# Column transform of a two-axis DFT computed for half of the rows, the mirrored rows summed from the same PSUM tiles read backwards

## The chip, the cores and the metric

The kernel runs on one core of one Trainium2 chip. The metric is the device time of one execution in microseconds (us), the median of three runs. TensorE is called PE below, VectorE DVE, ScalarE ACT, GpSimd POOL and SyncE SP. ACT, POOL and SP also issue DMAs[...].

## The reference, cut to what matters

Chunked attention (32 rows a chunk, 16 rows of left and 8 of right context, 8 memory rows) gives x of shape 4 x 768 x 512. A Fourier mixing and an MLP follow:

```
X = np.fft.fft(x, axis=1)
X = np.fft.fft(X, axis=2)
mixed = np.real(X).astype(np.float32)
u = x + mixed
mu = np.mean(u, axis=-1, keepdims=True)
var = np.mean((u - mu) ** 2, axis=-1, keepdims=True)
un = (u - mu) / np.sqrt(var + 1e-06)
ch = np.maximum(un @ w_ch1, 0.0) @ w_ch2
return (u + ch).astype(np.float32)
```

x is real, so row 768-k of `mixed` is row k with its 512 columns read as j -> (512-j) mod 512. The change rests on this.

## The kernel before, in words

A batch b (0 to 3) is 768 rows, six tiles of 128 rows, held in `xsb` (three buffers, so batch 3 waits until batch 0 is written out). Each batch has four attention units (two heads each), in all sixteen units n = 0 to 15. One unit loads q, k and v (`e_load_q` L242, `e_load_k` L247, `e_load_v` L252, all on SP), casts q and k (`e_cast_q` L270, `e_cast_k` L274: on DVE in batch 0, on POOL afterwards), copies the overlapping v rows (`e_overlap` L278, POOL), transposes on PE (L286, L302), takes scores (`e_scores` L316), exponentials on ACT (L331), values (`e_values` L335) and normalises into `xsb` on DVE (`e_norm` L351). The q, k and v buffers are for three units.

When a batch's x is complete, the row transform follows: folds on DVE (`zy`, `pq`, `ff`, L371 to L388), a split into a high and a low fp16 part (L396 on ACT, L401 on DVE), matmuls with cosine and sine tables (`ps`, L411), and a second split into `up` (L423 on ACT, L427 on DVE). `up` holds the 385 rows 0 to 384. `e_dn` (L430) copies it backwards on DVE into `dn`, which gives rows 384 to 767. The column transform is `e_columns` (L435): eight matmuls of 256 columns for each of six row tiles, from `up` for tiles 0 to 2 and from `dn`, with the sine table of the other sign, for tiles 3 to 5. `e_sum` (L447) adds the result to x in place; then come the statistics (L455, L456), `un` on ACT (L461), a transpose (`tp`, L468) and `unT` on DVE (L473), tile by tile.

The MLP of a batch runs in two halves of three tiles: sixteen blocks `ph` (L489, four matmuls each, one ReLU L496 on ACT each), then three blocks `pc` (L503, sixteen matmuls each), the sum `osb` on DVE (L509) and a store issued from ACT (`e_out` L512). The first `ph` of a half needs the three `unT` of that half. The two `ph`/`pc` PSUM buffers (`mlp`) alternate; `acc`, with two buffers as well, is shared by `ps`, `pm` and `tp`. The 4 MB of MLP weights are loaded by eight DMAs from POOL (L637, L639) once unit 3 is done.

What comes when is decided before the kernel is built: class `Plan` walks through all tasks with a hand-written cost each, gives every engine the first task by rank whose inputs and buffers are free at that planned time, and emits the tasks in the order so found. On the chip every engine then takes its instructions strictly in that order. MLP tasks have the lowest rank (`MLPS`), so PE takes them when it plans nothing else. SP takes its tasks in rank order and stops at the first that isn't ready.

Of the kernel before, what the change touches and what calls it, by code (L numbers as in the profile page):

```python
# [34 lines left out]
class Plan:  # L35
# [10 lines left out]
    def add(self, engine, cost, emit, after=(), take=(), give=(), rank=None, moved=0.0):  # L46
        t = dict(engine=engine, cost=cost, emit=emit, after=[a for a in after if a is not None],
                 take=take, give=give, rank=len(self.tasks) if rank is None else rank,
                 moved=moved, done=None, at=None, no=len(self.tasks))
        self.tasks.append(t)  # L50
        return t

    def order(self):
# [8 lines left out]
        while any(waiting.values()):  # L62
# [4 lines left out]
            for e, ts_ in waiting.items():  # L67
                if idle.get(e, 0.0) > now:
                    continue
                for t in ts_:  # L70
                    if any(a["done"] is None or a["end" if a["engine"] == e else "done"] > now
                           for a in t["after"]):
                        if e == "SP":
                            break
                        continue
                    need = {}
                    for tag in t["take"]:
                        need[tag] = need.get(tag, 0) + 1
                    if any(self.free[tag] < m for tag, m in need.items()):
                        if e == "SP":  # L80
                            break
                        continue
                    for tag in t["take"]:
                        self.free[tag] -= 1
                    cost = t["cost"] * (2.0 if e == "PE" and now < 40.0 else 1.0)
                    idle[e] = t["end"] = now + cost
                    if t["moved"]:
                        wire = max(wire, now + cost) + t["moved"]
                        t["done"] = t["end"] = wire + self.LAG["DMA"]
                    else:  # L90
                        t["done"] = now + cost + self.LAG.get(e, 0.07)
                    for tag in t["give"]:
                        gives.append((t["done"], tag))
                    t["at"] = now
                    placed.append(t)
                    ts_.remove(t)
                    moved = True
                    break
# [11 lines left out]
def kernel(  # L110
# [35 lines left out]
    fpool = ctx.enter_context(tc.tile_pool(name="fx", bufs=1))  # L146
    aps = ctx.enter_context(tc.tile_pool(name="attn_ps", bufs=1, space=bass.MemoryType.PSUM))
# [15 lines left out]
                     xsb=3, fold=2, hl=1, up=4, dn=4, acc=2, mlp=2, un=3, unT=2, hT=1, osb=3))  # L163
# [24 lines left out]
    NEG = -BIGM / 8.0  # L188
    cosS = wpool.tile([P, 2, 3, NK], FP16)
# [3 lines left out]
    sinD = wpool.tile([P, 2, HD], FP16)  # L193
# [225 lines left out]
    def e_up(b, par, ab):  # L419

        up = fpool.tile([P, 2, NK, 2], FP16, tag="up", bufs=4, name="up")
        up_of[b, par, ab] = [up.rearrange("p i k s -> p i (k s)"), None, up]
        nc.scalar.copy(up[:, 0].rearrange("p k s -> p s k"), ps_of[b, par, ab])  # L423

    def e_rest(b, par, ab):
        up = up_of[b, par, ab][2]
        nc.vector.tensor_tensor(up[:, 1].rearrange("p k s -> p s k"), ps_of.pop((b, par, ab)),  # L427
                                up[:, 0].rearrange("p k s -> p s k"), ALU.subtract)

    def e_dn(b, par, ab):  # L430
        dn = fpool.tile([P, 2, HS], FP16, tag="dn", bufs=4, name="dn")
        nc.vector.tensor_copy(dn, rev_ap(up_of[b, par, ab][2], HS, HS, [[2 * NK, 2]]))
        up_of[b, par, ab][1] = dn

    def e_columns(b, kt):  # L435
        pm_of[b, kt] = pm = fps.tile([P, 2, HD], FP32, tag="acc", name="pm")
        for par in range(2):
            im = 0
            for ab in range(2):
                rhs = cosD if ab == 0 else (nsinD if kt < 3 else sinD)  # L440
                for part in range(2):
                    lhs = up_of[b, par, ab][kt // 3][:, part, ts(kt % 3, P)]
                    nc.tensor.matmul(pm[:, par, :], lhs, rhs[:, par, :],  # L443
                                     start=(im == 0), stop=(im == 3))
                    im += 1

    def e_sum(b, kt):  # L447
        uv = xs[b][:, kt, :].rearrange("p (j c) -> p c j", c=2)
        nc.vector.tensor_tensor(uv, pm_of.pop((b, kt)), uv, ALU.add)  # L449

    def e_stats(b, kt):
# [3 lines left out]
        nc.vector.bn_stats(st6, xs[b][:, kt, :])  # L455
        nc.vector.bn_aggr(mu_of[b][:, kt, :], st6)  # L456

    def e_un(b, kt):
        un_of[b, kt] = un = fpool.tile([P, DM], FP16, tag="un", bufs=3, name="un")

        nc.scalar.activation(un, xs[b][:, kt, :], AFT.Identity, bias=mu_of[b][:, kt, 0:1],  # L461
# [17 lines left out]


# [25 lines left out]
    def e_osb(b, sh, stl):  # L506
# [3 lines left out]
                                       xs[b][:, st, :], ALU.mult, ALU.add)  # L510

    def e_out(b, st):  # L512
        nc.scalar.dma_start(out[b, ts(st, P), :], osb_of.pop((b, st)))


# [40 lines left out]
    t_norm = {}  # L556

# [53 lines left out]
    def e_sines(par):  # L611
# [4 lines left out]
        else:  # L616
            nc.scalar.activation(nsinD, rD, AFT.Sin, bias=0.0, scale=-scD)
            nc.scalar.activation(sinD, rD, AFT.Sin, bias=0.0, scale=scD)
            nc.scalar.activation(cosD, yD, AFT.Sin, bias=hpi_b, scale=-scD)

    def e_table_rows():

        for tab, par, s0 in ((nsinD, 0, 1.0), (sinD, 0, 1.0), (nsinD, 1, -1.0), (sinD, 1, 1.0)):
# [7 lines left out]
    t_sines = add("ACT", 6.2, e_all_sines, [t_angle["S"], t_angle["D"], x_last])  # L631
    t_rows = add("DVE", 1.3, e_table_rows, [t_sines])
# [10 lines left out]
    def fourier(b):  # L643
        nrm = [[t_norm[b * HP + i, g] for i in ii for g in range(2)] for ii in ((0, 1), (2, 3))]
        t_rest, t_dn = {}, {}
# [25 lines left out]
        for par in range(2):  # L671
            for ab in range(2):
                t_dn[par, ab] = add("DVE", 0.36, lambda par=par, ab=ab: e_dn(b, par, ab),
                                    [t_rest[par, ab]], take=("dn",))
# [4 lines left out]
        def columns(kt):  # L679
            cols[kt] = add("PE", 0.9, lambda: e_columns(b, kt),  # L680
                           allr + [t_rows] + (list(t_dn.values()) if kt > 2 else []),
                           take=("acc",),
                           give=("up",) * 4 if kt == 2 else ("dn",) * 4 if kt == 5 else ())
# [3 lines left out]
        for kt in range(NST):  # L687
            if kt + 1 < NST:
                columns(kt + 1)
            su = add("DVE", 0.7, lambda kt=kt: e_sum(b, kt), [cols[kt]], give=("acc",))  # L690
            sa = add("DVE", 0.9, lambda kt=kt: e_stats(b, kt), [su, sa])
            un = add("ACT", 0.72, lambda kt=kt: e_un(b, kt), [sa], take=("un",))
            tp = add("PE", 0.26, lambda kt=kt: e_turn_u(b, kt), [un, t_idh], take=("acc",),
                     give=("un",))
            t_un[kt] = add("DVE", 0.43, lambda kt=kt: e_unT(b, kt), [tp, t_un.get(kt - 1)],
                           take=("unT",) if kt == 0 else (), give=("acc",))
# [5 lines left out]
    def mlp(b, t_un, rs):  # L702
        for sh in range(2):
# [11 lines left out]
            for stl in range(3):  # L715
# [12 lines left out]
                add("ACT", 0.1, lambda st=st: e_out(b, st), [os_], give=("osb",), moved=0.9,  # L728
# [46 lines left out]
```

The softmax here doesn't subtract the row's maximum and nothing guards it: scores larger than these inputs give would overflow.

## Time and profile before

| what | us |
|---|---|
| three runs | 342.72, 344.65, 345.95; median 344.65 |
| span of the profiled execution | 342.6 |
| PE busy in it | 292.4 (85%) |
| DVE, ACT, POOL busy | 190.6, 168.9, 82.2 |
| matmuls `pm` (L443) | 192 of 256 columns |
| DVE copies `dn` (L432) | 16 of 455 ns, 7.1 |
| first `ph` of batch 0 (L489) starts | 77.98 |
| last DMA of the loads before the traffic ebbs | about 88 |

The median of the runs is 2.05 us above the span of the profile. PE, PEld (its weight loads) and the other engines overlap, so busy times don't add up to the span; a group's "idle before" is the time its engine stood still just ahead of it, with what ended that.

### The profile page before, as it was taken

To read this page: it belongs to the slowest core of one execution; us is meant where nothing else is said; L and a number is where in the kernel's file an instruction comes from. 1 tells how busy PE (TensorE), PEld (TensorE's weight loads), DVE (VectorE), ACT (ScalarE), POOL (GpSimd) and SP (SyncE) were. 2 spreads that over 40 slices of the span, in tenths; PEclk is the share of its full clock that TensorE was granted. 3 is DMA by queue.
4 is the path that set the end of the run, shared out by engine and by line. 5 is a ranking of instruction groups with operands and counts; after the bars stand their busy time and mean duration, and the time that the engine had idled before them with its cause. 6 is when DMAs were issued, how large, how long until landed. Compare 5 with 4: busy or idle time off the path is not lost.

```text
span 342.6 us, 6911 instructions
## 1 busy us (share of the span) xinstructions
PE 292.4 (85%) x2833; PEld 188.3 (55%) x2833; DVE 190.6 (56%) x374; ACT 168.9 (49%) x297; POOL 82.2 (24%) x89
## 2 busy tenths in 40 slices
PE   0678647959998886859999998699999999999995
PEld 0567535837555575637765665565645454554542
DVE  6954497958079999799793459860720100101001
ACT  7554784656737458674632733347226053160620
POOL 6534694233442736362001100000010000000000
PEclk9999999969999999998999999699999999999999
DMA  7999999999505893670002300010020100201001
GB/s 157 209 176 164 158 230 205 217 168 174 83 0 148 140 186 96 181 170 2 2 0 92 56 2 0 31 63 0 0 95 0 63 31 0 92 2 61 33 31 61
DMA packets 42046, 30.65 MB, mean 89 GB/s; under 512 B 30240, under 2 KB 32288, under 8 KB 42016
## 3 DMA queue, kind: packets, MB, share of 16 engines
q1 hardware_dynamic: 35584, 19.67, 32.5%
q0 software_dynamic: 2688, 4.19, 6.7%
q10 hardware_dynamic: 3744, 6.36, 4.8%
q8 instruction: 22, 0.36, 0.5%
q14 instruction: 8, 0.07, 0.1%
HBM read 28.11 MB, written 6.29 MB: 100 GB/s over the span
## 4 chain that ended last, share of the span: by engine, by line
PE 63%; DVE 16%; DMA 8%; SPq 3%; ACT 3%; issue 3%; POOL 3%; ACTq 0%; POOLq 0%
PE ph L489 23%; PE pc L503 22%; PE xa L347 6%; DMA qf<-in_q_dram 5%; PE pm L443 5%; PE ps L411 4%; DMA kf<-in_k_dram 2%; SPq L259 2%; DVE lo L401 2%; DVE zy L371 1%; PE tp L468 1%; DVE pq L379 1%; ACT e L331 1%; PE sc L323 1%; DVE xsb L358 1%
## 5 line engine op out<-in xcount | busy, mean ns | idle before, releaser
L496 ACT ACTIVATE hT<-ph 128x384 f16<-128x384 f32 x128 | 61.1, 492 | 73.2 <-PE ph L489 71.8
L489 PE MATMUL ph<-unT,w_sb 128*128 128x384 f16 x512 | 91.2, 326 | 1.4 <-ACT hT L496 0.8
L503 PE MATMUL pc<-w_sb,hT 128*128 128x512 f16 x384 | 88.3, 381 | 0.0
L489 PEld LDWEIGHTS <-w_sb 128*128 128x128 f16 x512 | 48.4, 97 | 36.8 <-issue 6.5
L509 DVE SCALAR_TENSOR_TENSOR osb<-pc,rstd,xsb 128x512 f32<-128x512 f32 x24 | 17.9, 748 | 83.2 <-PE pc L503 83.2
L503 PEld LDWEIGHTS <-hT 128*128 128x128 f16 x384 | 36.8, 98 | 40.0 <-issue 0.7
L280 POOL COPY va<-va 32x780 f32<-32x780 f32 x32 | 37.4, 1177 | 48.3 <-DMA va<-in_v_dram 40.8
L331 ACT ACTIVATE e<-sc,mbias 128x384 f32<-128x384 f32 x64 | 33.7, 579 | 22.5 <-PE sc L323 21.2
L347 PE MATMUL xa<-va,e 128*64 128x65 f32 x768 | 34.6, 250 | 7.9 <-ACT e L331 3.7
L347 PEld LDWEIGHTS xa<-va,e 128*64 128x64 f32 x768 | 29.9, 159 | 14.7 <-issue 7.2
L461 ACT ACTIVATE un<-xsb,mu_s 128x512 f16<-128x512 f32 x24 | 17.3, 722 | 22.4 <-DVE mu_s L456 22.3
L357 DVE RECIPROCAL zs<-xa 128x6 f32<-128x6 f32 x32 | 6.1, 192 | 32.7 <-PE xa L347 32.7
L477 POOL TENSOR_SCALAR rstd<-mu_s 128x6 f32<-128x6 f32 x4 | 1.0, 242 | 96.9 <-DVE osb L509 89.5
L323 PE MATMUL sc<-qT,kTb 64*128 64x64 bf16 x384 | 12.7, 206 | 11.8 <-ACT kTb L312 10.5
L423 ACT CAST up<-ps 128x386 f16<-128x386 f32 x16 | 9.7, 605 | 20.9 <-PE ps L411 19.5
L411 PE MATMUL ps<-cosS,hi 128*128 128x193 f16 (+1 forms) x72 | 16.8, 284 | 3.2 <-DVE ff L388 3.2
L411 PE MATMUL ps<-cosS,lo 128*128 128x193 f16 (+1 forms) x72 | 16.5, 284 | 3.1 <-DVE lo L401 3.1
L449 DVE TENSOR_TENSOR xsb<-pm,xsb 128x512 f32<-128x512 f32 x24 | 16.3, 678 | 4.1 <-PE pm L443 3.9
L358 DVE TENSOR_TENSOR xsb<-xa,zs 128x384 f32<-128x384 f32 x32 | 17.8, 558 | 1.1
L401 DVE TENSOR_TENSOR lo<-ff,hi 128x768 f16<-128x768 f32 x16 | 17.3, 1103 | 1.5 <-ACT hi L396 1.4
L323 PEld LDWEIGHTS <-kTb 64*128 64x128 bf16 x384 | 8.7, 103 | 17.1 <-ACT kTb L312 11.7
L396 ACT CAST hi<-ff 128x768 f16<-128x768 f32 x16 | 13.1, 832 | 9.8 <-DVE ff L388 9.7
(90 smaller groups left out, 374.6 us busy)
## 6 DMA issues: line engine op xcount, KB each, us to landing
qf<-in_q_dram SPq DMA_DIRECT2D x16, 384.0 KB, 4.2
kf<-in_k_dram SPq DMA_DIRECT2D x16, 384.0 KB, 4.1
out_dram<-osb ACTq DMA_DIRECT2D x24, 256.0 KB, 2.0
va<-in_v_dram SPq DMA_DIRECT2D x32, 144.0 KB, 4.7
w_sb<-in_moe_w_ch_dram POOLq DMA_DIRECT2D x8, 512.0 KB, 16.8
va<-in_v_dram SPq DMA_DIRECT2D x32, 48.0 KB, 7.2
va<-in_mem_v_dram SPq DMA_DIRECT2D x32, 24.0 KB
mkf<-in_mem_k_dram ACTq DMA_DIRECT2D x2, 32.0 KB, 3.7
```

The source lines that it names most:

```text
L280: nc.gpsimd.tensor_copy(v1[96:128, 0:NT, 0:D + 1], v1[0:32, 1:NB, 0:D + 1])
L323: nc.tensor.matmul(sc[:, hh, t6, :], kT[r0:r0 + 64, t * BS:t * BS + P], qT[r0:r0 + 64, ts(t, 64)], start=True, stop=True, tile_position=(r ...
L331: nc.scalar.activation(e1[:, :, :, ts(half, 32)], sc[:, :, 0:6, ts(half, 32)], AFT.Exp, bias=mbias[:, half:half + 1], scale=1.0 / math.sqr ...
L347: nc.tensor.matmul(xa[64 * half:64 * half + 64, st, hh, 0:65], e1[:, hh, t6, :], v1[:, 6 * g + t6, 0:65], start=True, stop=True)
L358: nc.vector.tensor_tensor(xs[b][:, 3 * g:3 * g + 3, 2 * pr * D:(2 * pr + 2) * D] .rearrange("p s (h d) -> p s h d", h=2), xa[:, :, :, 0:D] ...
L401: nc.vector.tensor_tensor(lo[:, ab].rearrange(fl), ff_of[b, par][:, ab].rearrange(fl), hi[:, ab].rearrange(fl), ALU.subtract)
L411: nc.tensor.matmul(out_[:, sp, :], part[:, ab, sp * 3 + st, c0:c1], tab[:, sp, st, :], start=(st == 0 and i == 0), stop=(st == 2 and i == 1))
L461: nc.scalar.activation(un, xs[b][:, kt, :], AFT.Identity, bias=mu_of[b][:, kt, 0:1], scale=-1.0)
L489: nc.tensor.matmul(ph[:, 0:384], w1_sb[:, dt, ts(ht, P)], unT_of[b][:, dt, sh * 384:(sh + 1) * 384], start=(dt == 0), stop=(dt == NDT - 1))
L496: nc.scalar.activation(hT_of[b, sh][:, ht, :], ph_of.pop((b, sh, ht))[:, 0:384], AFT.Relu, bias=0.0, scale=-1.0)
L503: nc.tensor.matmul(pc_of[b, sh, stl], hT_of[b, sh][:, ht, ts(stl, P)], w2_sb[:, ht, :], start=(ht == 0), stop=(ht == NHT - 1))
L509: nc.vector.scalar_tensor_tensor(osb, pc_of.pop((b, sh, stl)), rstd_of[b][:, st:st + 1], xs[b][:, st, :], ALU.mult, ALU.add)
```

## The change

- `columns` runs for three row tiles (m = 0 to 2), not six. `e_dn` and its buffers go, and so do the table `sinD`, its ACT instruction and four of the eight memsets on DVE.
- `e_middle` is new: eight matmuls with one column of weights, for row 384 alone.
- Mirrored tiles 3 to 5 take the `pm` of tile 0 to 2 backwards in `e_sum`, plus a one-column add for column 0, and for the first of them a one-row add for row 384. Row p of such a tile is now row 768 - 128 m - p of the output.
- x of those rows is brought into that order through DRAM: `e_mirror_out` stores tiles 3 to 5 of `xsb` (0.79 MB) from SP, `e_mirror_in` gathers them by three indexed DMAs from POOL into `xr` (one buffer). The index tile is built once on POOL (`e_turn`).
- Half of the output stores become scatters from POOL.
- Tiles are worked in the order KT = 0, 3, 1, 4, 5, 2. SP tasks marked `loose` may overtake a blocked SP task in the plan.

```diff
@@ class Plan, order()
+                held = False
                 for t in ts_:
+                    if held and not t["loose"]:
+                        continue
...
-                        if e == "SP":
-                            break
+                        held = held or (e == "SP" and not t["loose"])
                         continue
@@ column transform
-    def e_dn(b, par, ab):
-        dn = fpool.tile([P, 2, HS], FP16, tag="dn", bufs=4, name="dn")
-        nc.vector.tensor_copy(dn, rev_ap(up_of[b, par, ab][2], HS, HS, [[2 * NK, 2]]))
-        up_of[b, par, ab][1] = dn
+    def e_mirror_out(b):
+        fold_dram[b] = dr = dpool.tile([HS, DM], FP32, tag=f"mirror{b}", name=f"mirror{b}")
+        nc.sync.dma_start(dr.rearrange("(m p) d -> p m d", p=P), xs[b][:, 3:6, :])
+
+    def e_mirror_in(b):
+        xr_of[b] = xr = fpool.tile([P, 3, DM], FP32, tag="xr", bufs=1, name="xr")
+        for m in range(3):
+            nc.gpsimd.indirect_dma_start(
+                xr[:, m, :], None, fold_dram[b],
+                bass.IndirectOffsetOnAxis(ap=turn[:, 0, m:m + 1], axis=0))
...
+    def e_middle(b):
+        pm_of[b, 3] = pm = fps.tile([P, 2, HD], FP32, tag="acc", name="pm")
+        for par in range(2):
+            im = 0
+            for ab in range(2):
+                rhs = cosD if ab == 0 else nsinD
+                for part in range(2):
+                    nc.tensor.matmul(pm[0:1, par, :], up_of[b, par, ab][0][:, part, HS:HS + 1],
+                                     rhs[:, par, :], start=(im == 0), stop=(im == 3))
+                    im += 1
...
     def e_sum(b, kt):
-        uv = xs[b][:, kt, :].rearrange("p (j c) -> p c j", c=2)
-        nc.vector.tensor_tensor(uv, pm_of.pop((b, kt)), uv, ALU.add)
+        m = kt % 3
+        if kt < 3:
+            uv = xs[b][:, kt, :].rearrange(cj, c=2)
+            nc.vector.tensor_tensor(uv, pm_of[b, m], uv, ALU.add)
+            return
+        xr, pm = xr_of[b], pm_of[b, m]
+        turned = bass.AP(tensor=pm.tensor, offset=pm.offset + HD,
+                         ap=[list(pm.ap[0]), [HD - 1, 2], [-1, HD]])
+        nc.vector.tensor_tensor(xs[b][:, kt, :].rearrange(cj, c=2), turned,
+                                xr[:, m, :].rearrange(cj, c=2), ALU.add)
+        nc.vector.tensor_tensor(xs[b][:, kt, 0:1], pm[:, 0, 0:1], xr[:, m, 0:1], ALU.add)
+        if m == 0:
+            nc.vector.tensor_tensor(xs[b][0:1, kt, :].rearrange(cj, c=2),
+                                    pm_of.pop((b, 3))[0:1],
+                                    xr[0:1, m, :].rearrange(cj, c=2), ALU.add)
@@ stores
     def e_out(b, st):
-        nc.scalar.dma_start(out[b, ts(st, P), :], osb_of.pop((b, st)))
+        osb, kt = osb_of.pop((b, st)), KT[st]
+        if kt < 3:
+            nc.scalar.dma_start(out[b, ts(kt, P), :], osb)
+            return
+        nc.gpsimd.indirect_dma_start(
+            out.rearrange("b s d -> (b s) d"),
+            bass.IndirectOffsetOnAxis(ap=turn[:, 1 + b, kt - 3:kt - 2], axis=0), osb, None)
@@ fourier(b)
-        for par in range(2):
-            for ab in range(2):
-                t_dn[par, ab] = add("DVE", 0.36, lambda par=par, ab=ab: e_dn(b, par, ab),
-                                    [t_rest[par, ab]], take=("dn",))
+        mo = add("SP", 0.35, lambda: e_mirror_out(b), nrm[0] + nrm[1], moved=2.6, loose=True)
+        mi = add("POOL", 3.0, lambda: e_mirror_in(b), [mo, t_turn], take=("xr",), moved=2.6)
...
         columns(0)
-        for kt in range(NST):
-            if kt + 1 < NST:
-                columns(kt + 1)
-            su = add("DVE", 0.7, lambda kt=kt: e_sum(b, kt), [cols[kt]], give=("acc",))
+        cols[3] = add("PE", 0.7, lambda: e_middle(b), [cols[0]], take=("acc",))
+        for i, kt in enumerate(KT):
+            if kt == 3:
+                columns(1)
+            if kt == 4:
+                columns(2)
+            m = kt % 3
+            more = [] if kt < 3 else [mi] + ([cols[3]] if m == 0 else [])
+            su = add("DVE", 0.7 if kt < 3 else 1.5 if m == 0 else 0.8, lambda kt=kt: e_sum(b, kt),
+                     [cols[m]] + more,
+                     give={0: (), 1: (), 3: ("acc", "acc"), 4: ("acc",), 5: ("xr",),
+                           2: ("acc",)}[kt])
```

## The prediction

> **What bounds the kernel now.** I read the page's busy line first, then PE's busy time by stage, then the timeline of the first 100 us with the DMA view. PE is busy for 85% of the span, and time ends with it:
>
> ```profile
> PE 292.4 (85%) x2833; PEld 188.3 (55%) x2833; DVE 190.6 (56%) x374; ACT 168.9 (49%) x297; POOL 82.2 (24%) x89
> ```
>
> So span = PE's work + PE's idle time: 292.4 + 50.2 = 342.6. The stages show where it idles (columns: stretch, its length, busy time of each engine, clock, DMA share, GB/s):
>
> ```profile
> 0.00:78.20 78.20, 48.46 (x694) 39.92 (x695) 55.10 (x138) 48.06 (x72) 38.98 (x47) 0.96 1.10 187
> 78.20:135.60 57.40, 51.97 (x680) 35.39 (x678) 45.51 (x83) 34.65 (x60) 26.38 (x27) 1.00 0.64 119
> 135.60:175.00 39.40, 33.34 (x400) 24.59 (x397) 34.67 (x58) 24.47 (x44) 11.98 (x10) 0.96 0.32 78
> 175.00:202.80 27.80, 27.61 (x328) 16.94 (x326) 13.89 (x30) 13.10 (x26) 3.25 (x4) 1.00 0.17 46
> 202.80:229.00 26.20, 21.96 (x145) 14.30 (x143) 23.35 (x40) 8.19 (x13) 0.00 (x0) 0.87 0.05 21
> 229.00:342.60 113.60, 109.09 (x596) 57.20 (x595) 18.12 (x31) 40.38 (x83) 1.59 (x2) 0.99 0.10 38
> ```
>
> Idle: 29.7, 5.4, 6.1, 0.2, 4.2, 4.5. Six tenths of it lies ahead of 78.2, where the MLP of batch 0 starts. Until then PE has only attention and one row transform, and these wait for loads: the DMA share is 1.10. After 78.2 there is always MLP work to fill with. PE's timeline around that point (start, length, what, [idle before]):
>
> ```profile
> 73.58 0.82 PE L286 MATMUL trq<-ident_b,qb 96*128 96x96 bf16 x8 [3.73 <-POOL qb L272]
> ...
> 77.98 1.02 PE L489 MATMUL ph<-unT,w_sb 128*128 128x384 f16 x4
> ```
>
> The first waits for the q of unit 7; the second is the first MLP block. In the DMA view for 55 to 60 us the queue of POOL (weights, q0) and that of SP (q1) move equal numbers of packets:
>
> ```profile
> q0 software_dynamic: 620, 0.83, 91.8%
> q1 hardware_dynamic: 619, 0.15, 23.2%
> ```
>
> **What the Trainium skill says.** "DMA: Bandwidth & Descriptors", section "Queues, rings and completion order": each DMA engine takes turns between queues packet by packet. The 620 against 619 agree. The same page, "Anatomy of one DMA — SWDGE (gpsimd) path", prices a DMA from POOL at about 2.0 us + bytes / 436 GB/s; no indexed DMA is in this trace. "SBUF — State Buffer", "SBUF: two separate sides": a DVE instruction with two SBUF inputs and a POOL instruction that reads SBUF exclude each other. The trace agrees: `pq` (L378) takes 0.95 us alone at 52.10 and 1.67 at 98.62, beside POOL's cast at 98.22.
>
> **The change, part by part.**
>
> *PE.* In the chain that ended last a row tile's eight `pm` matmuls take 0.87 us (at 169.35, for one). Per batch three tiles go and `e_middle` comes. Its weights are one column wide, but so are the one-row `ps` matmuls, and these start every 0.085 us (12 from 108.15 to 109.08), as fast as the full ones before them. So `e_middle` costs a full 0.87: 4 x (3 - 1) x 0.87 = 7.0 us less. PE's work becomes 285.4.
>
> *DVE, ACT.* Sixteen `dn` copies go (7.1 us), with four memsets (0.165 each) and one sine (0.61, ACT). Added per batch: three one-column adds at about 0.18 (the 128x2 statistics row: 182 ns) and a one-row add of 512 elements at about 0.68 (`e_sum`'s own 678 ns), 1.2 us. Reading PSUM backwards I take as free: `ff`, which reads one operand backwards, needs 944 ns for 762 elements, `zy` 957 for 768; between 0 and double (0.68 x 12 = 8 us of DVE). Net 0.6 us less DVE per batch, too little to count.
>
> *DMA.* 4 x 0.79 MB out and in again. From batch 1 on the DMA share is 0.64 and falling; each later `xr` is ready before its `e_sum`: the row transform between them takes some 20 us. On SP these stores wait for the last `e_norm` of their batch with the loads behind them held: batch 1's before the second v of unit 10, batch 2's before that of unit 13 (units 13 to 15 are needed only after 187 us), batch 3's last of all; I cost that at nothing, and a late unit 10 at the most its transposes, 1 to 2 us. Only batch 0's meet full queues, which ebb at 88 us. In the built order its store stands on SP between the v loads of unit 6's two heads, issued at 44.62 and 45.78; x of batch 0 is done by then (its last `e_norm` starts at 40.71). At some 220 GB/s (the DMA view from 45 to 70 us), 0.79 MB is 3.6 us by which everything behind it on SP is late: v of unit 6, then q, k, v of units 7 and 8. The gather stands on POOL behind the overlap copy at 61.93, its packets behind the weights, which leave q0 at about 71. It shares turns with the loads of units 7 and 8: 3.6 us more for these. Its own landing: 2.6 us (estimate from the skill's price, 0.26 MB each) to 16.8 (median of the weights); I take about 81 us on the clock. POOL's issue I take as 1 us each (the weights' 0.62 to 0.80, plus indices; 0.6 to 2 possible). Behind it on POOL wait unit 6's second overlap copy and the casts of unit 7, and PE's `xa` of unit 6 for these.
>
> *The order.* This decides. On DVE, the mirrored sum of tile 3 now stands behind the last `e_norm` of unit 7 and a `zy` of batch 1. On PE, attention work stands ahead of the first `ph` that stood behind it before: five `xa` groups, five `sc`, two `trq`, three `trk`, about 10 us, less one `pm` group. So PE has done 48.5 + 9 = 57.5 us of work when the first `ph` comes. When is that? k of unit 7 was cast at 75.70; 5 us late, its transposes are at 81; copy 0.85, `sc` 0.45, exponentials 1.06, twice, end at 85.3; v of unit 7 is 7 us late, so its overlap copies end at about 85 too. `xa` and `e_norm` for both halves: 88.3; `zy`: 89.3. Then on DVE, up to `unT` of the third tile in the new order: tile 3 (0.68 + 0.18 + 0.68 + 0.88), `unT` 0.41, `pq` 1.9, tile 1 (1.56), tile 4 (1.74), `unT` 0.41, the sum of tile 5 (0.86), `unT` 0.41: 9.7, so 99 us. The first `ph` starts at 99 where it started at 78, with 99 - 57.5 = 41.5 us of PE idle by then, against 29.7.
>
> Does the deferred MLP fill later gaps? Little. Batch 1's row transform is bound by DVE (14.3 of 15 us busy in 110 to 125), starts about 6 us earlier but now carries 8.6 us of batch 0's sums, and ends near 132 as it did at 133.5. Only 16 `ph` and attention stand beside it on PE, 28.7 us of work in 33: idle 4.6 (5.4 before). Batch 2's has no `ph` between its four `ps` groups where before twelve stood: from the first `lo` to the last, DVE needs about 9 us (two `zy`, `pq`, `ff`, `lo`) for 4 of PE's; with 2 us on either side I take 9 for 6.1. Batch 3 and the tail keep 0.2 + 4.2 + 4.5.
>
> *Stores.* A plain store lands 2.0 us after its issue (DMA issues). A scatter lands 2.6 + 1 = 3.6 us after, with bounds 2.7 and 5. Each store now waits for the store before it, as the built order's waits show; tile 2's, on ACT, waits for tile 5's scatter, and the next half's ReLUs stand behind it. Stores of a half are 3.5 us apart (16 x 0.216), and ACT can be late by about 0.8 before `ph` runs out of its two buffers. So free at 3.6; beyond 4.3 the excess is paid up to twice a half.
>
> Sum: 285.4 + 41.5 + 4.6 + 9 + 0.2 + 4.2 + 4.5 = 349.4 span. The median of the runs stood 2.05 above the span; less rounding, 351.
>
> **The rivals.**
> A, the case above: 351, range of its own 347 to 356.
> B, the work saved shows in full: the lateness of PE's start is made up, because loads shift by little and DVE reaches tile 3 before 85. For it: gather and store together are only 7.2 us of DMA, and q0 empties at 71. Against: the order of DVE and PE alone puts unit 7 ahead of the first `ph`. 344.65 - 7.0 = 338. Faster than before, it decides if the first `ph` comes before 86 us: 57.5 + 29.7 = 87, where idle is as before.
> C, half of it: first `ph` near 93 and batch 2 filled as before: idle up by 6 to 7, the saving eaten, 345.
> D, the scatter: 5 us from issue to landing, so that ACT waits about 0.7 us more at each of the halves and twice where two scatters follow each other: some 12 x 0.7 = 8 us on top of A, 359. For it: POOL must read 128 indices, which nothing here shows. It decides from 4.3 us on.
> That the change does not do what it says is out: the built order has 64 `pm` pairs of weight load and matmul fewer.
>
> **How the numbers follow.** B 0.14, C 0.23, A 0.45, D 0.18. Predicted is A's 351. The range 341 to 361 leaves out most of B and the far end of D, and takes in a backwards PSUM read at double price in C. By 1% (what a measurement of this kernel can tell from no change; 341.2 and 348.1): faster 0.14 (B), same 0.22 (C, nearly all), slower 0.64 (A, D).
>
> **What would show it.** Right: `pm` 96 + 32 matmuls in all, PE busy near 285; first `ph` at 95 to 103; PE idle up to it about 41; `unT` or `xsb` waiting for unit 7, not for the gather; equal spacing of MLP halves in the tail (21.6 us). Wrong: first `ph` before 88 (B), a mirrored sum that waits for `xr` on DVE, ReLUs that wait for a store in the tail (D), a mirrored sum far from 0.68 us.

## The result, and the profile after

The changed kernel takes 376.0 us (median of four runs, 375.06 to 376.8) where the kernel before takes 345.05: a ratio of 1.0894 (95% interval 1.0831 to 1.0957). Slower was forecast, but 351 with a range of 341 to 361: the time lies 15 us above it. Below, a median is over all runs and a ratio leaves out those that ran slow, so that the two need not agree to the last digit.

The page of the changed kernel, busy line and granted clock by slice (before: PE 292.4 of 342.6):

```profile
PE 296.2 (79%) x2769; PEld 187.2 (50%) x2769; DVE 187.4 (50%) x370; ACT 168.4 (45%) x296; POOL 108.5 (29%) x123
...
PEclk9999997865789999979999699999996999999999
```

64 matmuls fewer, and PE is busy longer and idle for 78.7 us instead of 50.2. Where? The changed kernel by stage (stretch, its length, busy time of PE, PEld, DVE, ACT, POOL, clock, DMA share, GB/s):

```profile
0.00:102.70 102.70, 60.63 (x904) 49.37 (x905) 64.44 (x149) 56.15 (x84) 49.90 (x70) 0.87 1.12 189
102.70:137.60 34.90, 29.84 (x381) 21.91 (x378) 32.67 (x62) 24.61 (x45) 21.42 (x18) 0.95 0.68 144
137.60:200.30 62.70, 55.72 (x498) 33.92 (x499) 41.29 (x75) 28.77 (x50) 17.20 (x15) 0.95 0.32 78
200.30:210.90 10.60, 2.86 (x37) 1.76 (x35) 2.09 (x5) 1.04 (x3) 5.29 (x6) 0.85 0.35 94
210.90:235.00 24.10, 24.10 (x270) 14.31 (x270) 12.51 (x23) 11.98 (x24) 2.46 (x2) 0.92 0.14 47
235.00:276.80 41.80, 36.94 (x243) 22.16 (x241) 24.72 (x48) 15.59 (x28) 2.75 (x3) 0.96 0.11 37
276.80:286.50 9.70, 2.02 (x12) 0.98 (x11) 0.70 (x1) 1.02 (x3) 3.68 (x4) 0.81 0.15 56
286.50:374.90 88.40, 84.09 (x436) 42.82 (x435) 9.01 (x12) 29.21 (x62) 5.76 (x6) 0.98 0.10 39
```

The first line ends where the first `ph` starts, at 102.76 (99 forecast): 42.1 us idle (41.5 forecast). Two short stretches were in no forecast: of 10.6 and 9.7 us PE works 2.9 and 2.0. The list of waits of the changed kernel names what ended them (engine and line waited for: us in all, times, longest):

```profile
POOL rstd L513 <- DVE zs L360: 32.8, 1, 32.8
...
POOL rstd L513 <- DVE osb L547: 31.1, 1, 31.1
...
ACT hT L534 <- DMA out_dram<-osb,turn: 16.9, 2, 8.9
PE ph L527 <- ACT hT L534: 16.5, 6, 7.6
```

Read it from the bottom: PE waits for a ReLU, the ReLU for a scatter, 8.9 us at the longest. Why the scatter is late stands in POOL's timeline of the changed kernel (start, length, what, [idle before]), ACT's and PE's below it:

```profile
167.21 1.02 POOL L555 DMA_INDIRECT out_dram<-osb,turn  x1 [4.34 <-DVE osb L547]
201.07 0.25 POOL L513 TENSOR_SCALAR rstd<-mu_s 128x6 f32<-128x6 f32 x1 [32.84 <-DVE zs L360]
201.41 1.36 POOL L514 TENSOR_TENSOR rstd<-rstd,mhalf 128x6 f32<-128x6 f32 x1
202.98 1.10 POOL L555 DMA_INDIRECT out_dram<-osb,turn  x1 [0.21 <-issue]
207.10 0.97 POOL L555 DMA_INDIRECT out_dram<-osb,turn  x1 [3.02 <-DMA out_dram<-osb,turn]
```

```profile
209.97 0.34 ACTq L553 DMA_DIRECT2D out_dram<-osb  x1
210.35 0.87 ACT L534 ACTIVATE hT<-ph 128x384 f16<-128x384 f32 x2 [8.92 <-DMA out_dram<-osb,turn]
```

```profile
210.89 1.44 PE L527 MATMUL ph<-unT,w_sb 128*128 128x384 f16 x4 [7.55 <-ACT hT L534]
```

`rstd` of batch 2 stands on POOL ahead of two scatters of batch 0. It has two buffers, so it waits until batch 0's is read for the last time, by the last `osb` of batch 0; the profile puts the wait down to a neighbour on DVE. Only then come 1.6 us of `rstd`, the first scatter, the second that waits for the first to land, and ACT's plain store that waits for the second: 8.9 us in series with ReLUs behind them. At 277 us the same happens with batches 3 and 1. In the kernel before the same `rstd` waited longer still, in two waits, and cost nothing, because no store stood on POOL:

```profile
POOL rstd L477 <- DVE osb L509: 89.5, 2, 60.3
```

### The profile page after: what moved, and what is told of

Same layout as the page of the kernel before. It is cut to its first block, busy times and chain, and to the rows that moved or that the text cites. A ratio compares the mean times of both kernels' runs of the same rounds, so it can differ in the third digit from the quotient of the medians.

```text
span 374.9 us, 6830 instructions
## 1 busy us (share of the span) xinstructions
PE 296.2 (79%) x2769; PEld 187.2 (50%) x2769; DVE 187.4 (50%) x370; ACT 168.4 (45%) x296; POOL 108.5 (29%) x123
## 4 chain that ended last, share of the span: by engine, by line
PE 55%; DMA 20%; DVE 12%; ACT 5%; POOL 3%; issue 2%; SPq 1%; ACTq 1%; POOLq 0%; DVEq 0%
PE pc L541 21%; PE ph L527 19%; DMA kf<-in_k_dram 17%; PE xa L350 5%; PE ps L414 5%; DMA out_dram<-osb,turn 2%; PE pm L453 2%; DVE ff L391 2%; ACT e L334 2%; DVE lo L404 1%; DVE pq L382 1%; DVE st L491 1%; DVE zy L374 1%; PE sc L326 1%; DMA qf<-in_q_dram 1%
## 5 line engine op out<-in xcount | busy, mean ns | idle before, releaser
L527 PE MATMUL ph<-unT,w_sb 128*128 128x384 f16 x512 | 93.5, 332 | 17.1 <-ACT hT L534 16.5
L527 PEld LDWEIGHTS <-w_sb 128*128 128x128 f16 x512 | 49.7, 99 | 54.9 <-issue 25.3
L547 DVE SCALAR_TENSOR_TENSOR osb<-pc,rstd,xsb 128x512 f32<-128x512 f32 x24 | 17.8, 746 | 93.1 <-PE pc L541 93.1
L350 PE MATMUL xa<-va,e 128*64 128x65 f32 x768 | 38.0, 263 | 15.1 <-ACT e L334 6.6
L350 PEld LDWEIGHTS xa<-va,e 128*64 128x64 f32 x768 | 32.9, 172 | 23.0 <-ACT e L334 8.9
L283 POOL COPY va<-va 32x780 f32<-32x780 f32 x32 | 30.4, 952 | 41.1 <-DMA va<-in_v_dram 32.6
L555 POOL DMA_INDIRECT out_dram<-osb,turn x12 | 11.9, 993 | 98.3 <-DVE osb L547 84.3
L442 POOL DMA_INDIRECT xr<-mirror,turn x12 | 14.9, 1240 | 28.3 <-DMA mirror<-xsb 25.7
L414 PE MATMUL ps<-cosS,lo 128*128 128x193 f16 (+1 forms) x72 | 17.5, 296 | 3.8 <-DVE lo L404 3.8
L426 ACT CAST up<-ps 128x386 f16<-128x386 f32 x16 | 9.6, 601 | 22.2 <-PE ps L414 22.2
L275 POOL CAST qb<-qf 96x1024 bf16<-96x1024 f32 x12 | 15.9, 1324 | 11.3 <-DMA qf<-in_q_dram 8.6
L279 POOL CAST kb<-kf 104x1024 bf16<-104x1024 f32 x12 | 16.8, 1399 | 6.9 <-DMA kf<-in_k_dram 5.9
```

What stands on the lines that cost most here:

```text
L275: eng.tensor_copy(qb_of[n].rearrange(cp_b), qf[n % NS].rearrange(cp_q, j=RB))
L279: eng.tensor_copy(kb_of[n].rearrange(cp_b), kf[n % NS].rearrange(cp_q, j=RB))
L283: nc.gpsimd.tensor_copy(v1[96:128, 0:NT, 0:D + 1], v1[0:32, 1:NB, 0:D + 1])
L350: nc.tensor.matmul(xa[64 * half:64 * half + 64, st, hh, 0:65], e1[:, hh, t6, :], v1[:, 6 * g + t6, 0:65], start=True, stop=True)
L414: nc.tensor.matmul(out_[:, sp, :], part[:, ab, sp * 3 + st, c0:c1], tab[:, sp, st, :], start=(st == 0 and i == 0), stop=(st == 2 and i == 1))
L527: nc.tensor.matmul(ph[:, 0:384], w1_sb[:, dt, ts(ht, P)], unT_of[b][:, dt, sh * 384:(sh + 1) * 384], start=(dt == 0), stop=(dt == NDT - 1))
```

## The experiments

Each was measured beside the kernel before on the same chip; the median of that was 345 to 346.6 us in all of them. Not all variants ran on the same chip, so the ratios compare better than the medians.

**1. Take the hold away.** Two ways: more buffers, or stores that are not on POOL.

```diff
-  rstd = fpool.tile([P, NST], FP32, tag="rstd", bufs=2, name="rstd")
+  rstd = fpool.tile([P, NST], FP32, tag="rstd", bufs=4, name="rstd")
```

> The changed kernel, but the tile of the row statistics (rstd, written by POOL) has four buffers where it had two; nothing else differs and the order on each engine stays. Theory H (the scatters of a batch's second half stand on POOL behind the rstd of batch b+2, which waits for the last osb of batch b): the two stretches at 200 to 211 and 277 to 287 us, 7.7 us of idle PE each, go; no ReLU waits more than 1 us for a store; 376 - 15.4 = 361 us (358 to 363). Theory D (the scatter itself takes too long): the ReLU waits stay, 374 to 377. Where the granted clock stays at about 0.93, PE's busy time stays near 296; if it was low because of the two stretches, the clock goes up to 0.96 or more and the time falls below 357.

```diff
-        if kt < 3:
-            nc.scalar.dma_start(out[b, ts(kt, P), :], osb)
-            return
-        nc.gpsimd.indirect_dma_start(
...
+        nc.scalar.dma_start(out[b, ts(kt, P), :], osb)
```

> The changed kernel, with rstd at two buffers, but all stores plain ones issued from ACT; the mirrored tiles are written in the order in which they lie in SBUF, so their rows in the output are not turned back (left out: the permutation of half of the output rows). Theory H: nothing stands behind rstd on POOL any more, so the same 15 us go: 359 to 363, within 2 us of the kernel with four rstd buffers. Theory D: plain stores save more than the four buffers do, 354 or less here while the four buffers leave 374 to 377. If both show 361, a scatter in its place costs what a plain store costs.

Measured: four buffers 359.3 us (ratio to before 1.037, interval 1.0286 to 1.0454), plain stores 360.9 (1.0412, 1.0368 to 1.0456). The two stretches with four buffers:

```profile
200.30:210.90 10.60, 10.41 (x153) 6.64 (x152) 4.62 (x10) 6.99 (x15) 1.97 (x3) 1.00 0.40 94
276.80:286.50 9.70, 9.70 (x51) 4.79 (x50) 0.75 (x1) 3.25 (x7) 0.00 (x0) 1.00 0.07 24
```

PE is all but full, and no ReLU waits for a store any more. The hold costs 16.7 us by the medians and 18 by the ratios (1.0894 - 1.037), and plain stores save no more than the buffers do: a scatter that is issued in time costs nothing that these runs can tell. That the scatter itself is too slow has fallen.

**2. Take the trip of x away, first alone, then from the plan too.** In the first, store and gather emit nothing and the sums read x where it lies; in the second the plan's two tasks have no engine and no cost:

```diff
-        mo = add("SP", 0.35, lambda: e_mirror_out(b), nrm[0] + nrm[1], moved=2.6, loose=True)
-        mi = add("POOL", 3.0, lambda: e_mirror_in(b), [mo, t_turn], take=("xr",), moved=2.6)
+        mo = add("NONE", 0.0, lambda: e_mirror_out(b), nrm[0] + nrm[1], loose=True)
+        mi = add("NONE", 0.0, lambda: e_mirror_in(b), nrm[0] + nrm[1], take=("xr",))
```

> Four rstd buffers, and the trip of x through DRAM left out: no store of tiles 3 to 5, no gather, and the mirrored sums read x where it lies (left out: x of the mirrored rows is not turned, so their sums are of the wrong rows). The order of all other instructions is that of the changed kernel. Theory O (the late first ph comes from the order on DVE and PE): the first ph stays at 97 to 103 and the time within 4 us of the kernel with four rstd buffers, 357 to 361. Theory T (it comes from the trip's DMA traffic and waits, 0.8 MB each way while the loads saturate the queues): the first ph comes 5 us or more earlier, and the time is 352 to 355.

> As the kernel without the trip, but the plan does not know of the trip either, so that it orders the work as it did before the change: the mirrored sums of batch 0 stand no longer behind unit 7 on DVE, and MLP blocks stand among the attention work on PE. Left out as there: x of the mirrored rows is not turned. Theory O: first ph before 88 us, PE idle up to it near 30 us, and the saved column work shows in full: 336 to 342 us at a clock of 0.97. Theory T: no better than the kernel without the trip by more than 2 us, 350 to 355. If the granted clock is the cause of PE's longer busy time and doesn't depend on the order, 5 to 10 us more in either case.

Measured: 357.3 (1.0333, 1.0279 to 1.0387) and 347.3 (1.0000, 0.9968 to 1.0033). In the profiled executions the first `ph` starts at 102.6 with the trip, at 95.9 without it, at 80.5 in the new order. Without the traffic the first `ph` comes 7 us earlier, as theory T had it, but the median is only 2 us less, which the intervals don't tell from none. Part of the 7 us may be the execution: the profiled one without the trip was the fastest of four, 3 us below their median. The order gives 10 us. But the second half of what was expected failed: with the first `ph` at 80.5 the time is that of before, not 336 to 342. The 7.0 us of PE work are not to be seen.

The other way round, the trip kept and planned as taking no time:

```diff
-        mo = add("SP", 0.35, lambda: e_mirror_out(b), nrm[0] + nrm[1], moved=2.6, loose=True)
-        mi = add("POOL", 3.0, lambda: e_mirror_in(b), [mo, t_turn], take=("xr",), moved=2.6)
+        mo = add("SP", 0.0, lambda: e_mirror_out(b), nrm[0] + nrm[1], loose=True)
+        mi = add("POOL", 0.0, lambda: e_mirror_in(b), [mo, t_turn], take=("xr",))
```

> Four rstd buffers, the whole trip of x, but the plan counts it as taking no time, so the mirrored sums of batch 0 stand on DVE ahead of the attention work of unit 7. The gather of batch 0 lands at about 81 us in the runs so far and tile 3 stands on DVE at about 72: theory O+T (either the sums stand behind unit 7, or DVE stands still for the gather) expects the first ph at 88 to 92 and 352 to 357. If the gather needs 17 us only because it is not waited for, first ph before 86 and 348 to 350. If DVE's stop holds up attention too, 358 or more.

Measured: 377.9 us (1.1026, 1.0941 to 1.1111), 21 to 26 above what theory O+T expected, though the first `ph` at 89.2 was as it expected. The expectation had given 358 or more to a stop of DVE. POOL's timeline of this kernel shows that another engine stops:

```profile
62.57 1.07 POOL L442 DMA_INDIRECT xr<-mirror,turn  x1 [10.85 <-DMA mirror<-xsb]
...
120.59 1.10 POOL L442 DMA_INDIRECT xr<-mirror,turn  x1 [21.95 <-DMA mirror<-xsb]
```

POOL stands 10.9 and 22.0 us at the gathers of batches 0 and 1 until the mirror store has landed, with the v copies and casts of the following units behind it. PE in turn waits up to 10.9 us for the cast of k (`trk` L305) and 12.4 us for a v copy (`xa` L350). The same mistake as in the prediction, made again: an instruction put on a queue was priced without what it holds up there.

**3. The replanned kernel without its scatters.** Edit as in the plain stores above.

> As the replanned kernel without the trip, but all stores plain ones from ACT (left out: the turning of x and the turning back of the mirrored rows in the output). In the replanned kernel one scatter stands on POOL behind the rstd of batch 2 and PE stands 3.3 us at 183.8 for it. Theory H: that wait goes, with the clock that drops after it: 342 to 344, 3 to 5 us less. If the wait is no more than one of several that take each other's place, no change beyond 1.5 us.

Measured: 342.3 (0.9901, 0.9864 to 0.9938), less by 5.0 in the medians and by 1% (3.4 us) in the ratios, as expected. So the hold takes another form there: in the replanned kernel `rstd` of batch 2 starts at 181.30, when its own statistics are done, the scatter stands behind it at 183.19, and PE waits 3.3 us for the ReLU behind that. Once it is gone, 3.3 us of the 7.0 can be seen against the kernel before.

**4. What is the work worth in its place?** In the kernel before, with all waits and the order kept: without 64 of the `pm`; then without `dn`.

```diff
-                    nc.tensor.matmul(pm[:, par, :], lhs, rhs[:, par, :],
-                                     start=(im == 0), stop=(im == 3))
+                    if kt < 3 or im == 0 or (kt == 5 and im == 3):
+                        nc.tensor.matmul(pm[:, par, :], lhs, rhs[:, par, :],
+                                         start=(im == 0), stop=(im == 3 or kt in (3, 4)))
```

> The kernel before the change, with 64 of its 192 column matmuls pm left out (those of tiles 3 to 5, which get a part of their sums only), as many as the change takes away; dn, all waits and the order on each engine stay as they are. It measures what this PE work is worth in its place. If time is PE's work plus its waits for others, which don't change, 7.0 us less: 339 to 341 where before stands at 346.5. If the column stages are bound by DVE and the freed PE time turns into idle time there, 344 to 346.5. My theory is the first for batches 1 and 2 and the second for batches 0 and 3, where no MLP block can fill: 341 to 343.

```diff
-        nc.vector.tensor_copy(dn, rev_ap(up_of[b, par, ab][2], HS, HS, [[2 * NK, 2]]))
-        up_of[b, par, ab][1] = dn
+        up_of[b, par, ab][1] = up_of[b, par, ab][0]
```

> The kernel before the change without its sixteen dn copies (7.1 us of DVE): tiles 3 to 5 take their weights from up forwards (left out: the turning, so rows 384 to 767 are wrong), all else in the same order. If DVE sets the pace of the column stages, 339 to 342 where before stands at 345.6, while the 64 pm left out gave nothing; if neither engine's work alone counts but the order of waits, 344 to 346.

Measured: 345.5 (1.0008, 0.9977 to 1.0038) and 344.0 (0.9955, 0.9929 to 0.9982). 64 `pm`, priced at 7.0 us, gone, and nothing gained, where 341 to 343 had been expected; 7.1 us of DVE work gone, 1.5 us gained. PE's timeline in the column stage of batch 1 shows where a part of the first went. Kernel before:

```profile
128.25 0.38 PE L443 MATMUL pm<-sinD,dn 128*128 128x256 f16 x2
128.56 0.35 PE L323 MATMUL sc<-qT,kTb 64*128 64x64 bf16 x12
128.84 0.54 PE L302 MATMUL trk<-ident_b,kb 104*128 104x104 bf16 x8
129.22 0.39 PE L468 MATMUL tp<-ident_h,un 128*128 128x128 f16 x4
130.12 0.38 PE L468 MATMUL tp<-ident_h,un 128*128 128x128 f16 x4 [0.51 <-DVE unT L473]
```

Without 64 `pm`:

```profile
127.14 0.38 PE L444 MATMUL pm<-cosD,dn 128*128 128x256 f16 x2 [0.22 <-DVE xsb L450]
127.46 0.35 PE L323 MATMUL sc<-qT,kTb 64*128 64x64 bf16 x12
128.15 0.53 PE L302 MATMUL trk<-ident_b,kb 104*128 104x104 bf16 x8 [0.34 <-ACT qT L291]
128.66 0.38 PE L469 MATMUL tp<-ident_h,un 128*128 128x128 f16 x4
129.92 0.38 PE L469 MATMUL tp<-ident_h,un 128*128 128x128 f16 x4 [0.87 <-DVE unT L474]
...
132.94 0.63 PE L469 MATMUL tp<-ident_h,un 128*128 128x128 f16 x4
```

PE reaches the scores 1.1 us earlier, and waits for ACT and DVE until the second `tp` starts at 129.92 instead of 130.12. Here the chain sum, statistics, `un`, `tp`, `unT` sets the pace, and in the fixed order freed PE time becomes waiting. Later the same transposes take 0.63 us instead of 0.38 to 0.40: the granted clock from 110 to 135 us is 0.90 here and 1.00 before. Over the whole execution PE is busy 4.0 us less than before (288.4) and idle 3.4 us more, at a clock of 0.925 instead of 0.973; the other executions of this kernel had mostly about 0.96 and took as long.

**5. Mirror only where the trip is free.** Batch 0 as before the change, batches 1 to 3 mirrored, `rstd` planned behind the last `unT` and with four buffers. `MIR = (1, 2, 3)` names the mirrored batches:

```diff
-        if kt < 3:
+        if kt < 3 or b not in MIR:
...
-        rs = add("POOL", 1.0, lambda: e_rstd(b), [sa])
+        rs = add("POOL", 1.0, lambda: e_rstd(b), [sa, t_un[5]])
```

> The whole computation: batch 0 as before the change (dn, six row tiles, plain stores), batches 1 to 3 by mirrored rows with the trip; four rstd buffers, and rstd planned behind the last unT of its batch. From the runs so far: order and traffic of the first 80 us as before, so no late first ph (78 to 80); 5.2 us of PE work less; no ReLU waits over 1 us. If the saved work shows, 340 to 343, faster than before by 1 to 2%; if the stages of the mirrored batches lose it again to waits on their sums (the two acc buffers are held by the pm that serve two tiles), 345 to 348.

Measured: 329.8 us (0.9571, 0.9514 to 0.9627). Faster than both kernels, and by 10 us more than expected. Why? Three controls of this kernel: `MIR = ()`; the `pm` of tiles 1 and 2 of batches 1 to 3 computed twice; a backwards copy behind each second split of batches 1 to 3:

```diff
+        for again in range(2 if b in MIR and m > 0 else 1):
...
+        if b in MIR:
+            scr = fpool.tile([P, 2, 336], FP16, tag="scr", bufs=1, name="scr")
+            nc.vector.tensor_copy(scr, rev_ap(up, HS, 336, [[2 * NK, 2]]))
```

> The kernel with batch 0 direct, but no batch mirrored: the whole computation as before the change (six row tiles, dn, plain stores), with what else that kernel has (four rstd buffers, rstd planned behind the last unT of its batch, the index tile built on POOL). If its 15.8 us come from the mirrored batches, 344 to 347 here; if they come from rstd's place or from another plan, 329 to 335.

> The kernel with batch 0 direct and batches 1 to 3 mirrored, but the pm matmuls of row tiles 1 and 2 of each mirrored batch run twice with the same result: 48 matmuls, 5.2 us of PE work, are back at the same places of the same order. If PE sets the pace there, 334 to 336; if these stages go at DVE's pace, as the kernel before without 64 pm suggests (no change there), 330 to 332, and the gain over before does not come from PE's work at all.

> The kernel with batch 0 direct and batches 1 to 3 mirrored, with twelve backwards copies (2 x 336 fp16, some 0.35 to 0.45 us each, 4 to 5 us of DVE in all) put back on DVE right behind the second splits, into a tile that nobody reads. If DVE sets the pace of the stages of batches 1 to 3, 333 to 336; if it has slack there, 329 to 331.

Measured: 344.9 (1.0001, 0.9979 to 1.0024), 333.5 (0.9669, 0.9627 to 0.971), 330.2 (0.9567, 0.9528 to 0.9607). So without a mirrored batch neither `rstd`'s place nor the index tile brings anything. 5.2 us of PE work put back cost some 3.7: the time lies between the two that were expected, and the intervals just touch. DVE's copies cost nothing that can be told. 15.8 - 3.7 - 0.4 = 11.7 us are left by this subtraction for neither engine's work. What remains to be tried is the order.

**6. The order without the mirror.** No batch mirrored, all computed as before the change, but tiles of batches 1 to 3 in the paired order and two costs of the plan set to nothing; then the same with the costs given back.

```diff
-    t_dn.append(add("DVE", 0.36, lambda par=par, ab=ab: e_dn(b, par, ab),
+    t_dn.append(add("DVE", 0.36 if b == 0 else 0.0, lambda par=par, ab=ab: e_dn(b, par, ab),
...
-    cols[m] = add("PE", 0.9,
+    cols[m] = add("PE", 0.9 if low or b == 0 else 0.0,
```

> No batch mirrored, the whole computation as before the change, but in batches 1 to 3 the row tiles are worked in the order 0, 3, 1, 4, 5, 2, and the plan counts dn and the columns of tiles 3 to 5 there as taking no time, so that it orders the rest about as it does where these batches are mirrored. If the unexplained 11 to 12 us of the kernel with batches 1 to 3 mirrored come from the order of the work, 333 to 338 here; if they need the mirrored sums themselves, 343 to 347.

> No batch mirrored; row tiles of batches 1 to 3 in the order 0, 3, 1, 4, 5, 2, but the plan counts dn and the columns of tiles 3 to 5 at their costs (0.36 and 0.9) again. If the 10.6 us of the kernel with the paired order and these costs at nothing came from the plan's costs, 343 to 346; if from the order of the tiles, 333 to 337.

Measured: 334.3 (0.968, 0.9631 to 0.9729), and 344.8 (1.0001, 0.9969 to 1.0033) with the costs given back. With the paired tiles, the order that the plan finds when it thinks these steps free is worth 10.6 us to the unchanged computation; the order of the tiles alone nothing. The two costs at nothing with the tiles in their old order were not run, and which of the tasks that stand elsewhere brings the gain was not taken apart. The kernel with batches 1 to 3 mirrored, whose order this one was to come near, stands at 329.8 against 334.3: some 4 us would then be the mirror's own, which agrees with the 3.7. From 96 to 215 us PE works so long; no batch mirrored, then with the two costs at nothing:

```profile
96.00:215.00 119.00, 105.62 (x1280) 71.76 (x1276) 97.33 (x167) 64.05 (x112) 36.32 (x32) 0.99 0.37 77
```

```profile
96.00:215.00 119.00, 109.90 (x1288) 72.37 (x1285) 97.62 (x171) 65.49 (x117) 36.04 (x32) 1.00 0.40 82
```

That stretch shows 4.3 us of the gain. Over these two executions, 342.8 and 331.7 us long, PE is idle for 7.0 us less, and busy for 4.1 us less with the same 2833 matmuls, at a granted clock of 0.995 instead of 0.978.

Which batches bring it, with the mirror:

> The whole computation, with batches 1 and 2 mirrored, 0 and 3 direct. The idle time that went lies between 96 and 205 us, the stages of batches 1 and 2 (17 us without a mirrored batch, 7 with three): nearly all of the 15 us should be here, 330 to 333. If the last batch's stage, where nothing can fill, brings a share as large as its 1.75 us of PE work and more, 333 to 337.

> The whole computation, with batch 3 alone mirrored. Its column stage has no attention work left to fill with, so what it saves is 1.75 us of PE work and less DVE: 342 to 344.5. If the gain lies in this batch, 336 or less.

`MIR = (1, 2)`: 327.6 (0.9462, 0.9411 to 0.9512), the fastest of all and below the 330 that were expected at the least; why batch 3 mirrored as well costs something there stays open. `MIR = (3,)`: 344.3 (0.997, 0.9934 to 1.0006), the 1.75 us of PE work of that batch hardly visible.

**7. The clock.** Filler matmuls of constants where PE stands still, in the changed kernel with four `rstd` buffers; the second time shorter and at the right wait:

```diff
+        e_warm(spare, 40 if (n, g) == (7, 0) else 0)
         for st in range(3):
             for hh in range(2):
+                if (st, hh) == (0, 1):
+                    e_warm(spare, 36 if (n, g) == (7, 0) else 0)
```

> The changed kernel with four rstd buffers, with matmuls of constants put where PE stands still between 76 and 92 us: 8 ahead of each trq and trk of units 6 to 8, 90 and 70 ahead of the first values of unit 6, into PSUM that is overwritten afterwards (the result is unchanged). In the kernel without them the granted clock is 0.50 from 80 to 96 us and matmuls there take 1.5 to 2 times as long. If the clock drops because PE stands still, it stays at 0.9 or more here; if that costs time, 353 to 357 instead of 359.3; if the matmuls in that stretch wait for loads anyway, the clock goes up and the time stays at 358 to 361.

> The changed kernel with four rstd buffers, with short filler matmuls of constants where PE waits in unit 7: 12 ahead of each of its score groups (waits of 0.9 and 1.2 us), 40 and 36 ahead of the two parts of its first values (waits of 3.2 and 2.9 us), into PSUM that is overwritten or never read (the result is unchanged). If the low clock costs time, the granted clock stays above 0.8 from 76 to 96 us, the pm and xa of that stretch take 0.38 and 0.92 us a group again, the first ph comes 1.5 to 3 us earlier than 102.6 and the time is 355 to 357.5. If the matmuls there wait for loads anyway, clock up but time 358.5 to 360.5. If the fillers themselves get in the way, first ph later than 103.5 and the question stays open.

Measured: 374.3 (1.0824, 1.0774 to 1.0873) and 360.1 (1.0422, 1.0351 to 1.0493). The first put its fillers in unit 6 instead of unit 7, and far too many: they held PE from 72 to 91 us, and the first `ph` came at 115.5. It shows one thing: the clock was 1.00 from 72 to 92 us, where it is 0.50 from 80 us on without them. The stretch of 80 to 84 us without fillers, then with the first ones (the clock is the third number from the end):

```profile
80.00:84.00 4.00, 0.49 (x4) 0.32 (x4) 0.00 (x0) 0.08 (x1) 0.00 (x0) 0.50 1.10 164
```

```profile
80.00:84.00 4.00, 4.00 (x74) 4.00 (x73) 0.00 (x0) 0.00 (x0) 0.18 (x1) 1.00 0.87 126
```

The second got the clock up from 84 to 92 only; the first `ph` came at 103.9, beyond the 103.5 up to which it was to decide anything. So what the low clock costs stays open. Two records above point different ways. In the profiled execution of experiment 4 without the 64 `pm`, the clock was 0.68 from 30 to 78 us (0.93 in the kernel before), and yet the first `ph` came at 76.6 (77.98): there, while PE waits for loads, the low clock cost nothing to be seen. And where PE idles less, as with the two costs at nothing, the same matmuls took 4.1 us less.

## Why the prediction was wrong, step by step

The forecast sum beside the changed kernel and the one with four `rstd` buffers, us:

| | forecast | changed | four buffers |
|---|---|---|---|
| PE work up to the first `ph` | 57.5 | 60.6 | 59.5 |
| PE idle up to it | 41.5 | 42.1 | 43.1 |
| PE work after it | 227.9 | 235.6 | 233.8 |
| PE idle after it | 22.5 | 36.6 | 22.2 |
| span | 349.4 | 374.9 | 358.6 |

**The step that failed: stores.** The forecast put the wait ahead of a scatter's issue at nothing; it cost 16.7 us. "Each store now waits for the store before it; tile 2's, on ACT, waits for tile 5's scatter, and the next half's ReLUs stand behind it. [...] So free at 3.6". The 3.6 were too long, on the harmless side. In the tail a scatter lands 2.7 us after its issue begins, with the 0.96 us of issue inside. The estimate of 2.6 from the price in the Trainium skill, "DMA: Bandwidth & Descriptors", section "Anatomy of one DMA — SWDGE (gpsimd) path", fits that as it stands, and the 1 us for the issue was added to it once too often. In the tail the scatters are free, as forecast: the first `osb` of the last halves stand 21.68, 20.9 and 20.71 us apart, 21.67, 20.91 and 20.7 before. The chain of waits was seen as well. What was not asked is what stands ahead of the scatter on POOL: the working counts the seconds from its issue on. In the built order `rstd` stands there, and its wait was in the list of waits of the kernel before, where it was harmless. This wait made 14.1 us more idle time after the first `ph` than forecast, and 16.7 us in the runs. Without it the time is 359.3, inside the range. Rival D had the right victim, "ReLUs that wait for a store", with the wrong place and price: the tail and 8 us.

**The second term: PE's work.** The 64 `pm` fewer and their 7.0 us were counted rightly (96 full ones and 32 of one row, each with 0.27 us in the median). PE was busy 296.2 us, 293.4 with four buffers, not 285.4. These 8 to 11 us go with the granted clock: 0.927 and 0.937, 0.973 before. From 80 to 96 us it is 0.50, and the same group of `xa` takes longer there than behind it:

```profile
89.52 1.57 PE L350 MATMUL xa<-va,e 128*64 128x65 f32 x24
...
98.53 0.92 PE L350 MATMUL xa<-va,e 128*64 128x65 f32 x24
```

The Trainium skill, "TensorE: Matmul & The Clock Gate", section "What's actually happening", says that PE's clock falls to half once it was idle for a window of some 3.4 us and comes back after as long of work. The trace agrees with the half (0.50), and the first filler run with the cause; the length of the window is not shown here. A forecast with 12 us more idle time up to the first `ph` (41.5 against 29.7) should have had slower matmuls too. How much of the 8 to 11 us is lost time is open: part of it lies where PE waits anyway.

**Rival B's premise came true, and not its price.** "It decides if the first `ph` comes before 86 us": it came at 80.5 in the replanned kernel, which took 347.3, not 338. Taking work off an engine that is busy for 85% pays only where that engine sets the pace. In the column stages of the order before it doesn't (0 of 7.0, to about 1 us either way), in the order of the last kernels it mostly does (some 3.7 of 5.2).

**What was right.** The order as the main cause of the late first `ph`, its time (99; 102.8), the idle time up to it, the idle time of the later stages (22.5; 22.2 without the hold). The trip: 2 us (not separable from none) on the time. The mirrored sum waits for unit 7 and not for the gather: in the changed kernel it starts at 92.84 right behind the `zy` that follows the last `e_norm`. The gather's landing at about 81 (in the four-buffer kernel 17.3 to 17.8 us after issues at 62.0 to 65.1). The backwards read: 672 ns in the median, 684 forwards.

So of 31 us, 16.7 are the hold, some 10 the order, 2 the trip (not told from none); of the 2 left over, 1.5 lie in the kernel before itself, which stood at 345.05 beside the changed one and at 346.56 beside these variants. The 7.0 that should have come off were not there to take in the order of the kernel before.

## What to carry to other kernels

When an operation moves to another queue, write down what stands ahead of it there and what that waits for, and what stands behind it: a wait that was free becomes a stall when something urgent is queued behind it. Before PE work is taken out, price it in its place: leave it out in the old kernel with the order kept; here that was worth nothing. And where a plan orders the work from costs, try other costs first: two of them set to nothing, with the tiles paired, gave 10.6 us without a change of the computation.

## What the runs showed of the hardware

- An indexed DMA from POOL of 0.26 MB takes 0.95 to 1.8 us to issue in the changed kernel (gather 1.24 on average, scatter 0.99). Counted from the start of the issue, a scatter lands after 2.7 us in the tail, a gather after 3.6 to 4.1, and the gathers of batch 0, among the loads, after 18.5 to 18.8.
- A PSUM operand read backwards on DVE costs what it costs forwards (672 against 684 ns for 128 x 512).
- The granted clock is 0.50 from 80 to 96 us in the changed kernel, where PE has waits of up to 3.1 us for loads and copies, and stays at 1.00 under filler matmuls. At 0.50 a pair of `pm` takes 0.63 us instead of 0.38.
